# The q projection of the first two token tiles taken from raw x, with LayerNorm applied to its sums

## The chip, the cores and the metric

One core of a Trainium2 chip runs the whole program. Its engines are TensorE (matmul and transpose, "PE"; its weight loads are listed as "PEld"), VectorE ("DVE"), ScalarE ("ACT"), GpSimd ("POOL") and SyncE ("SP", which here issues DMAs). The metric is the device time of one execution in microseconds, from runs on the chip; profiled executions add when each instruction ran.

## The reference

A transformer layer for 2048 tokens of width 1024, in bfloat16: `h = x + attention(LN(x))`, `out = h + gMLP(LN(h))`. What the change touches is the first step:

```python
def _layernorm(x, axis=-1, eps=1e-05):
    m = jnp.mean(x, axis=axis, keepdims=True)
    v = jnp.var(x, axis=axis, keepdims=True)
    return (x - m) / jnp.sqrt(v + eps)

# _A_ref(_layernorm(x), A_wqkv, A_wo): 32 heads of 32, a window of 8 positions in steps of 2
qkv = (x @ wqkv).reshape(B, S, 3, H, Dh)
logits = einsum('bhsd,bhswd->bhsw', q, kg) * Dh ** -0.5
attn = softmax(where(mask, logits, -1e9))
o = einsum('bhsw,bhswd->bhsd', attn, vg)
... o @ wo
```

The LayerNorm has no weights, so for a token with mean m and reciprocal deviation r, q = r * (x @ wq) - (r * m) * (column sums of wq).

## The kernel before

The 2048 tokens are 16 tiles of 128 (`P`), four to a chunk of 512 (`CH`, `TPC` = 4, chunks c = 0 to 3). The inner width 1024 is eight slices kt of 128 (`KT`); the outputs of q, k and v are eight groups dl (`DLO`). TensorE needs x with the width on the partitions, so every normalised tile is transposed: chunk 0 by TensorE (`xpose`, L279), the others by a DMA transpose (L416) from `xns` into `xnT`, of which the pool `xtp` (L191) has two buffers.

At the start (L208 to L238) TensorE runs `NWARM` dummy matmuls on a zeroed tile, while SP's queue loads in this order: half of each of tiles 0 and 1, wq in eight slices of 256 KB with tiles 2 and 3 behind the fifth, two pairs of tiles (2 and 3), wk, pairs 4 and 5, `xl` (the tiles of chunk 3) and wv. ScalarE's queue loads the other halves of tiles 0 and 1 and the constants `csb`: the identity for the transposes, `E32` (used at L527), `B4` (L589) and a mask. Pairs 4 and 5 use the buffers of pairs 0 and 1.

Then comes the first stage, written out in order (L319 to L350). For a tile, VectorE takes the statistics of both halves (`stats`, L241), ScalarE the root (`root`, L264), VectorE the reciprocal (`scale`, L315) and the normalised tile (`norm`, L269). TensorE transposes it, eight blocks of 128 x 128, into PSUM; ScalarE or VectorE copies it to `xnT[0]`. The q of tiles 0 and 1 is summed in two accumulators `qacc` by `q_left(k0, k1, lo, hi)`, for slices k0 to k1 and tiles lo to hi; `ALONE` = 5 slices are done for each tile alone, with 128 columns, while the next tile isn't there yet, and the rest for both, with 256. After L350 the q of tiles 2 and 3 is done with 256 columns (L353 to L358), and ScalarE writes all of it to `att_in[0][0]`, the q of chunk 0.

All that follows is put in order by `Order` (L64): each operation is added with an engine, an estimated duration, what it depends on and a priority, and `run` places them on a clock for each engine; the instructions are emitted in that order, so each engine runs its list in program order whatever the real times are. Its clocks start at the estimated end of the first stage: `{"PE": 22.9, "ACT": 24.1, "DVE": 15.4, "POOL": 12.0}` (L372). `slots` counts the buffers of some tags.

In this list: the LayerNorm of chunks 1 to 3 (`ln1`, L384: statistics on VectorE, a power on GpSimd at L405 for the reciprocal roots, the normalised tiles on VectorE, then the DMA transpose); k and v of chunk 0 and q, k and v of the others (`qkv`, L428, matmuls at L439 in units of four); and `attention` (L461). Attention of chunk 0 starts on VectorE with products of q and k (L497) and three steps of adding (L501, L504, L507). TensorE sums them over the heads' width into the scores with `E32` (L527), and the softmax follows on VectorE and ScalarE. `prod`, `part` and `ssum` are the tags of the tiles used there.

Of the kernel before, what the change touches and what calls it, by code (L numbers as in the profile page):

```python
# [29 lines left out]
EPS = 1e-5  # L30
SCALE = DH ** -0.5
NEG = -1.0e9
NWARM = 11
ALONE = 5
XRB = 3
LMODE = (1, 1, 1, 1)
LSLACK, BSLACK = 2.0, 0.3
# [5 lines left out]


def _consts():
    c = np.zeros((P, 128 + 32 + 128 + 128), np.float32)
    c[:, 0:128] = np.eye(P)
    for p in range(P):
        c[p, 128 + p // 4] = 1.0
    for k in range(P):  # L50
        h = k % 32
        c[k, 160 + 4 * h:160 + 4 * h + 4] = 1.0
    for w in range(W_WIN):
        for s in range(16):
            if s - DIL * w < 0:
                c[0:32, 288 + w * 16 + s] = NEG
    return c.astype(ml_dtypes.bfloat16)


# [68 lines left out]
def kernel(  # L128
# [31 lines left out]
    csb = cpool.tile([P, 416], BF16, name="csb")  # L160
    ident = csb[:, 0:128]
    E32 = csb[:, 128:160]
    B4 = csb[:, 160:288]
    maskb = csb[0:32, 288:416].rearrange("p (w s) -> p w s", w=W_WIN)
# [45 lines left out]
    wps = ps_tp.tile([P, CH], FP32, name="wps", tag="t0")  # L210
    for _ in range(NWARM):
        T.matmul(wps[:], warm[:, 0:P], warm[:], start=True, stop=True)
    V.memset(eps_t[:], EPS)
    V.memset(nhalf[:], -0.5)

    wsb = [wtile([P, KT, D], "wq", "wA"), wtile([P, KT, D], "wk", "wA"), wtile([P, KT, D], "wv", "wB")]
    with tc.manual_schedule(engines={mybir.EngineType.SP}):
        for i in range(TPC):
            x_slot(i)
        for i in range(2):  # L220
            for q_, lo in ((nc.sync, 0), (nc.scalar, CH)):
                q_.dma_start(xts[i][:, lo:lo + CH], x2d[i * P:(i + 1) * P, lo:lo + CH])
        A.dma_start(csb[:], consts_d.ap()[:, :])
        for kt in range(KT):
            dma(wsb[0][:, kt, :], wq_view[:, kt, 0:D])
# [12 lines left out]
        dma(wsb[2][:], wq_view[:, :, 2 * D:3 * D])  # L238
# [33 lines left out]
            V.tensor_scalar(xn[:, lo:hi], xts[i][:, lo:hi], mv1[:, i, 0:1], rstd1[:, i:i + 1], op0=ALU.subtract, op1=ALU.mult)  # L272
# [6 lines left out]
    def xpose(i, lo, hi, tag):  # L279
        ps = (ps_acc.tile([P, 2, 2 * CH], BF16, name="tpa", tag="acc")[:, 0] if tag == "acc" else  # L280
              ps_tp.tile([P, 2 * CH], BF16, name="tp" + tag, tag=tag))
        for a in range(lo, hi):
            T.transpose(ps[:, (a - lo) * P:(a - lo + 1) * P], xn[i][:, a * P:(a + 1) * P], ident)  # L283
        return lambda cp: cp(xnT[0][:, i, lo:hi, :], ps[:, 0:(hi - lo) * P].rearrange("p (a s) -> p a s", s=P))

    def q_mm(dst, dl, kt, lo, hi, start, stop):
        T.matmul(dst.rearrange("p (a b) -> p a b", b=P), wqs[:, kt, dl, :], xnT[0][:, lo:hi, kt, :], start=start, stop=stop)  # L287

    def q_left(k0, k1, lo, hi):
        for kt in range(k0, k1):  # L290
            for dl in range(DLO):
                c0 = (dl % 2) * 2 * P
                q_mm(qacc[dl // 4][:, dl % 4 // 2, c0 + lo * P:c0 + hi * P], dl, kt, lo, hi,
                     kt == 0 and lo == 0 and dl % 2 == 0, kt == KT - 1 and dl % 2 == 1)

    def q_half_out(half, lo, acc):
        A.copy(att_in[0][0][:, 4 * half:4 * half + 4, lo * P:(lo + 2) * P], acc[:].rearrange("p a (d s) -> p (a d) s", d=2))
# [30 lines left out]
    scale(1)
    xn[1] = norm(1, cuts=(0, CH, D))
    q_left(0, ALONE - 1, 0, 1)  # L330
    xpose(1, 0, 4, "t0")(A.copy)
    q_left(ALONE - 1, ALONE, 0, 1)
    xpose(1, 4, 8, "t1")(A.copy)
# [8 lines left out]
    q_left(0, ALONE, 1, 2)
    q_left(ALONE, ALONE + 1, 0, 2)
    xpose(2, 0, 4, "t0")(A.copy)
    xpose(2, 4, 8, "t1")(A.copy)
    q_left(ALONE + 1, KT - 1, 0, 2)
    xpose(3, 0, 4, "t0")(A.copy)
    xpose(3, 4, 8, "t1")(V.tensor_copy)
    q_left(KT - 1, KT, 0, 2)
    sm7 = sums_act(7, 0, junk())  # L350
    for half in range(2):
        q_half_out(half, 0, qacc[half])
    sums_act(7, 1, junk(), sm7)  # L353
    for half in range(2):
# [29 lines left out]
    def ln1(c):  # L384
        sts = []
        for il in range(TPC):
            i = c * TPC + il
            arrive = add("DMA", X_AT[c] + 0.8 * il, lambda: None)
            if il < TPC - 1 or c == 3:
                sts.append(add("DVE", 1.4, lambda i=i: stats(V, i), [arrive], prio=LNPRIO[c]))  # L390
                continue
            if c == 1:
                G["sm", c] = sm7
                sa = add("DMA", 19.0, lambda: None)
            else:
                def sums(i=i):
                    G["sm", c] = sums_act(i, 0, junk())
                    sums_act(i, 1, junk(), G["sm", c])
                sa = add("ACT", 2.4, sums, [arrive], prio=4.0, lat=0.2)
            sts.append(add("DVE", 0.45, lambda i=i: var_act(i, G["sm", c]), [sa], prio=LNPRIO[c]))  # L400
        def ve():
            G["ve", c] = l1.tile([P, TPC], FP32, name="ve1", tag="ve1")
            V.tensor_scalar(G["ve", c][:], mv1[:, c * TPC:(c + 1) * TPC, 1], EPS, None, op0=ALU.add)
        s1 = add("DVE", 0.15, ve, sts, prio=LNPRIO[c] - 0.5)
        r1 = add("POOL", 1.05, lambda: nc.gpsimd.tensor_tensor(rstd1[:, c * TPC:(c + 1) * TPC], G["ve", c][:], nhalf[:], op=ALU.pow),  # L405
                 [s1], lat=0.4)
# [566 lines left out]
```

## Time and profile before

| what | value |
|---|---|
| median of 3 runs | 724.17 us (724.12 to 726.06) |
| the profiled execution | 723.34 us |
| its span, first to last instruction | 721.6 us |
| TensorE's granted clock, mean | 1.000 |
| first real transpose on TensorE | 6.31 us |
| first matmul of k (L439) in the chain | 23.23 us |
| first product of attention 0 on VectorE (L497) | 39.76 us |
| POOL busy in the whole span | 51.2 us |

Times in the timeline are microseconds from the first instruction of the span. A line of it gives the start, the length, the engine, the line of the kernel, the operation and what it writes and reads; a bracket at the end is the idle time of the engine before it and what ended that. Lines of the chain give start, length and what was running. TensorE's matmuls are pipelined, so the length of one is more than the distance to the next; for the rate one divides a run of them by their number.

### The profile page before, as it was taken

What the parts mean: (1) busy time and instruction counts of PE and PEld (TensorE: products, weight loads), DVE (VectorE), ACT (ScalarE), POOL (GpSimd) and SP (SyncE); (2) the same over time, 40 slices, a digit from 0 to 9 for tenths busy, and PEclk for the clock granted to TensorE, in tenths of its full rate; (3) what the DMA queues carried; (4) which work ended last, traced back from release to release, by engine and by line L of the source; (5) the groups of instructions that cost most, each with busy time, mean ns of one, the idle gap of its engine ahead of it and who ended that gap; (6) DMA issues with size and microseconds to landing.
All of it is one profiled execution on the core that took longest, in us unless ns stands there. A gap on an engine that the chain in (4) does not pass through costs nothing.

```text
span 721.6 us, 8559 instructions
## 1 busy us (share of the span) xinstructions
PE 714.1 (99%) x3493; PEld 370.3 (51%) x3537; DVE 420.8 (58%) x470; ACT 217.7 (30%) x280; POOL 51.2 (7%) x61
## 2 busy tenths in 40 slices
PE   8999999999999999999999999999999999999998
PEld 7766665666545444445445444444444444444444
DVE  6899899999999799988951103222222222222222
ACT  4523432533348866738825420000000000000000
POOL 0100010012110111000204100000000000000000
PEclk9999999999999999999999999999999999999999
DMA  9964697389973594642849899163016411120002
GB/s 327 322 185 110 201 215 206 128 233 277 312 301 58 188 238 142 233 117 66 223 129 294 230 299 295 48 148 116 29 45 128 132 33 45 35 86 11 0 17 71
DMA packets 117590, 113.12 MB, mean 157 GB/s; under 512 B 68080, under 2 KB 95120, under 8 KB 117424
## 3 DMA queue, kind: packets, MB, share of 16 engines
q1 hardware_dynamic: 108528, 75.48, 35.7%
q0 software_dynamic: 8448, 36.64, 17.6%
q8 instruction: 27, 0.44, 0.3%
q10 hardware_dynamic: 576, 0.47, 0.2%
q14 instruction: 11, 0.09, 0.0%
HBM read 57.19 MB, written 31.26 MB: 123 GB/s over the span
## 4 chain that ended last, share of the span: by engine, by line
PE 98%; DMA 0%; DVE 0%; issue 0%; ACT 0%
PE acc L912 27%; PE acc L439 21%; PE acc L816 13%; PE acc L761 13%; PE acc L927 13%; PE acc L684 8%; PE acc L287 2%; DMA xp<-in_A_x_dram 0%; PE L L527 0%; PE tpt L283 0%; PE pb L589 0%; DVE bnst L242 0%; DVE xn L272 0%; DVE bnst L243 0%; PE tpa L283 0%
## 5 line engine op out<-in xcount | busy, mean ns | idle before, releaser
L912 PE MATMUL acc<-wspT,z2sb 128*128 128x512 bf16 x878 | 193.1, 379 | 0.9
L912 PEld LDWEIGHTS <-z2sb 128*128 128x128 bf16 x896 | 87.7, 98 | 105.7
L915 DVE TENSOR_TENSOR g<-acc,bB 128x1024 bf16<-128x1024 f32 x28 | 34.3, 1224 | 160.2 <-PE acc L912 127.9
L816 PE MATMUL acc<-hnT,win 128*128 128x512 bf16 x448 | 98.0, 379 | 0.0
L761 PE MATMUL acc<-win,hnT 128*128 128x512 bf16 (+1 forms) x501 | 97.4, 352 | 0.6
L761 PEld LDWEIGHTS <-hnT 128*128 128x128 bf16 x512 | 49.9, 98 | 47.5 <-issue 0.7
L497 DVE TENSOR_TENSOR prod<-qT,kT 128x4096 bf16<-128x4096 bf16 x32 | 72.4, 2283 | 0.0
L927 PEld LDWEIGHTS <-zg 128*128 128x128 bf16 x462 | 44.7, 98 | 52.4
L816 PEld LDWEIGHTS <-win 128*128 128x128 bf16 x448 | 43.7, 98 | 52.6 <-issue 0.7
L450 ACT CAST stg<-acc 128x1024 bf16<-128x1024 f32 x36 | 36.4, 1011 | 77.2 <-PE acc L439 66.4
L934 DVE TENSOR_TENSOR ot<-acc,hr 128x1024 bf16<-128x1024 f32 x15 | 18.4, 1225 | 69.4 <-PE acc L927 60.5
L927 PE MATMUL acc<-wout_a,zg 128*128 128x512 bf16 (+2 forms) x260 | 58.0, 373 | 0.3
L439 PE MATMUL acc<-xnT,wk 128*128 128x512 bf16 x256 | 56.5, 380 | 0.0
L439 PE MATMUL acc<-xnT,wv 128*128 128x512 bf16 x256 | 56.1, 380 | 0.0
L684 PE MATMUL acc<-wo_sb,av_oT 128*128 128x512 bf16 x250 | 55.6, 379 | 0.3
L439 PEld LDWEIGHTS <-wv 128*128 128x128 bf16 x256 | 36.7, 144 | 18.5 <-issue 0.2
L439 PEld LDWEIGHTS <-wk 128*128 128x128 bf16 x256 | 36.6, 144 | 18.7 <-issue 0.7
L927 PE MATMUL acc<-wout_b,zg 128*128 128x512 bf16 (+2 forms) x193 | 43.8, 373 | 0.2
L439 PE MATMUL acc<-xnT,wq 128*128 128x512 bf16 x192 | 42.1, 380 | 0.0
L684 PEld LDWEIGHTS <-av_oT 128*128 128x128 bf16 x256 | 25.0, 98 | 30.1
L822 ACT ACTIVATE z1s<-acc 128x1024 bf16<-128x1024 f32 x28 | 28.6, 1022 | 37.8 <-PE acc L816 33.5
L501 DVE TENSOR_TENSOR prod<-prod 128x2048 bf16<-128x2048 bf16 x32 | 38.4, 1217 | 0.1
(140 smaller groups left out, 562.1 us busy)
## 6 DMA issues: line engine op xcount, KB each, us to landing
qkv_d<-stg SPq DMA_DIRECT2D x36, 256.0 KB, 3.9
z_d<-z1s SPq DMA_DIRECT2D x28, 256.0 KB, 2.6
z1c<-z_d SPq DMA_DIRECT2D x28, 256.0 KB, 2.8
z_d<-u SPq DMA_DIRECT2D x12, 448.0 KB, 2.8
z2sb<-z_d POOLq DMA_DIRECT2D x12, 448.0 KB, 9.7
xr<-in_A_x_dram SPq DMA_DIRECT2D x16, 256.0 KB, 3.1
av_y<-av_z POOLq DMA_DIRECT2D x4, 1024.0 KB, 8.6
av_oT<-av_zz POOLq DMA_DIRECT2D x4, 1024.0 KB, 12.1
```

The source lines that it names most:

```text
L439: T.matmul(G[key][:, j, :].rearrange("p (a b) -> p a b", a=TPC), wv[:, kt, dl, :], xnT[c][:, :, kt, :], start=(kt == 0), stop=(kt == KT - 1))
L450: A.copy(stg[:], G[key][:])
L497: V.tensor_tensor(st["prod"][:], qT[:], kT[:, :, o:o + CH], op=ALU.mult)
L501: V.tensor_tensor(dst, p_[:, 0:4, :], p_[:, 4:8, :], op=ALU.add)
L684: T.matmul(st["acc", il][:, nh, :], oTs[c][:, dl, il * P:(il + 1) * P], wo_sb[:, dl, nh * CH:(nh + 1) * CH], start=(dl == 0), stop=(dl == ...
L761: T.matmul(accf[:, n0:n1], hnTs[c][:, il, kt, :], wins[hf][:, kt, n0:n1], start=(kt == 0), stop=(kt == KT - 1))
L816: T.matmul(G["accy", c, fp][:, j, :].rearrange("p (a b) -> p a b", a=TPC), wt[:, kt, f0 * P:(f0 + 1) * P], hnTs[c][:, :, kt, :], start=(kt ...
L822: A.activation(z1s[:], G["accy", c, fp][:], ACTF.Gelu_apprx_tanh)
L912: T.matmul(acc[:, j, :], z2sb[a][:, f * P:(f + 1) * P], wspT[:, a, :], start=(a == 0), stop=(a == NT - 1))
L915: V.tensor_tensor(g1[:], acc[:], bB[:, c * CH:(c + 1) * CH].unsqueeze(1).to_broadcast([P, 2, CH]), op=ALU.add)
L927: T.matmul(outs, zg[:, f, il * P:(il + 1) * P], wt[:, f0, lo:hi], start=(f == 0), stop=(f == NF - 1))
L934: V.tensor_tensor(ot[:], acc[:].rearrange("p a b -> p (a b)"), hr[:], op=ALU.add)
```

## The change

The constants lose the identity, which GpSimd now makes in place (a memset and an affine_select). `NWARM` goes from 11 to 6, `ALONE` from 5 to 2. The first tile comes in two halves on two queues as before; the second in one piece on SP's queue, behind the first slice of wq; the constants behind all of wq.

Tiles 0 and 1 are transposed as they come, into a tile `raw`, and the q of both is summed from it. They are normalised later and transposed again into `xT0`, which serves k and v. Their means and reciprocal deviations are written to DRAM and read back as rows, repeated on all partitions, in `mr`; all of these DMAs are on GpSimd's queue. ScalarE copies the sums to `qraw`. GpSimd multiplies mean by deviation, and `qraw` by the deviation. `xT0` has a column of ones behind the last token, so the q matmuls of tiles 2 and 3, 257 columns wide, also give wq's column sums (`csum`). Two operations in the ordered list, one for each half, multiply these with `mr[:, 0]` and subtract that from `qraw`, both on GpSimd, into `att_in[0][0]`.

`raw` and `xT0` are two tiles of the tag `xnT`, and `qraw` and `qcor` two of the tag `part`.

```diff
-NWARM = 11
-ALONE = 5
+NWARM = 6
+ALONE = 2
+XC = TPC * P + 4
...
+    nc.gpsimd.memset(ident[:], 0.0)
+    nc.gpsimd.affine_select(out=ident[:], in_=ident[:], compare_op=ALU.not_equal, fill=1.0, base=0, pattern=[[-1, P]], channel_multiplier=1)
...
-        for i in range(2):
-            for q_, lo in ((nc.sync, 0), (nc.scalar, CH)):
-                q_.dma_start(xts[i][:, lo:lo + CH], x2d[i * P:(i + 1) * P, lo:lo + CH])
-        A.dma_start(csb[:], consts_d.ap()[:, :])
+        for q_, lo in ((nc.sync, 0), (nc.scalar, CH)):
+            q_.dma_start(xts[0][:, lo:lo + CH], x2d[0:P, lo:lo + CH])
         for kt in range(KT):
             dma(wsb[0][:, kt, :], wq_view[:, kt, 0:D])
+            if kt == 0:
+                dma(xts[1], x2d[P:2 * P, :])
...
+        dma(csb[:], consts_d.ap()[:, :])
...
-    xnT[0] = xtp.tile([P, TPC, KT, P], BF16, name="xnT", tag="xnT")
+    xT0 = xtp.tile([P, KT, XC], BF16, name="xT0", tag="xnT")
+    V.memset(xT0[:, :, TPC * P:TPC * P + 1], 1.0)
+    xnT[0] = xT0[:, :, 0:TPC * P].rearrange("p a (t s) -> p t a s", s=P)
+    raw = xtp.tile([P, KT, XC], BF16, name="raw", tag="xnT")
...
+    def q_left(kt, lo, hi):
+        for dl in range(DLO):
+            c0 = (dl % 2) * 2 * P
+            T.matmul(qacc[dl // 4][:, dl % 4 // 2, c0 + lo * P:c0 + hi * P], wqs[:, kt, dl, :], raw[:, kt, lo * P:hi * P],
+                     start=(kt == 0 and lo == 0 and dl % 2 == 0), stop=(kt == KT - 1 and dl % 2 == 1))
...
-    stats(V, 0)
-    scale(0)
-    xn[0] = norm(0, cuts=(0, 2 * P, CH, D))
...
+    qacc.extend((new_acc(), new_acc()))
+    put = [xpose(xts[0], raw, 0, lo, lo + 4, tag) for lo, tag in ((0, "t0"), (4, "t1"))]
+    put[0](V.tensor_copy)
+    put[1](A.copy)
+    stats(V, 0)
+    q_left(0, 0, 1)
+    xpose(xts[1], raw, 1, 0, 4, "t0")(A.copy)
+    q_left(1, 0, 1)
+    xpose(xts[1], raw, 1, 4, 8, "t1")(A.copy)
     stats(V, 1)
...
+    sd0 = root(0, 2)
+    V.reciprocal(rstd1[:, 0:2], sd0[:, 0:2])
+    st_d = dpool.tile([2, 2 * P], FP32, name="st_d")
+    dma_w(st_d[0].rearrange("(t p) -> p t", p=P), mv1[:, 0:2, 0])
+    dma_w(st_d[1].rearrange("(t p) -> p t", p=P), rstd1[:, 0:2])
+    mr = att.tile([P, 2, 2 * P], FP32, name="mr", tag="ssum")
+    for k in range(2):
+        dma_w(mr[:, k, :], st_d[k].unsqueeze(0).to_broadcast([P, 2 * P]))
+    xn[0], xn[1] = norm(0), norm(1)
+    q_left(0, 1, 2)
+    q_left(1, 1, 2)
+    q_left(2, 0, 2)
+    q_left(3, 0, 2)
+    for i, tag in ((0, "t0"), (1, "t1")):
+        xpose(xn[i], xT0, i, 0, 8, tag)(A.copy)
+        q_left(4 + i, 0, 2)
     stats(V, 2)
     sd2 = root(2, 3)
...
+    q_left(6, 0, 2)
+    xpose(xn[2], xT0, 2, 0, 8, "t0")(A.copy)
+    q_left(7, 0, 2)
+    xpose(xn[3], xT0, 3, 0, 4, "t1")(V.tensor_copy)
+    xpose(xn[3], xT0, 3, 4, 8, "t0")(V.tensor_copy)
+    qraw = att.tile([P, DLO, 2 * P], FP32, name="qraw", tag="part", bufs=2)
+    qcor = att.tile([P, DLO, 2 * P], FP32, name="qcor", tag="part", bufs=2)
+    csum = l1.tile([P, DLO], FP32, name="csum", tag="csum")
+    for half in range(2):
+        A.copy(qraw[:, 4 * half:4 * half + 4, :], qacc[half][:].rearrange("p a (d s) -> p (a d) s", d=2))
+    nc.gpsimd.tensor_tensor(mr[:, 0, :], mr[:, 0, :], mr[:, 1, :], op=ALU.mult)
+    nc.gpsimd.tensor_tensor(qraw[:], qraw[:], mr[:, 1, :].unsqueeze(1).to_broadcast([P, DLO, 2 * P]), op=ALU.mult)
     sm7 = sums_act(7, 0, junk())
...
+    for dp in range(DLO // 2):
         acc = new_acc()
+        for j in range(2):
             for kt in range(KT):
+                T.matmul(acc[:, j, 0:2 * P + 1], wqs[:, kt, 2 * dp + j, :], xT0[:, kt, 2 * P:4 * P + 1], start=(kt == 0), stop=(kt == KT - 1))
+        A.copy(att_in[0][0][:, 2 * dp:2 * dp + 2, 2 * P:4 * P], acc[:, :, 0:2 * P])
+        A.copy(csum[:, 2 * dp:2 * dp + 2], acc[:, :, 2 * P])
+        if dp == 0:
+            sums_act(7, 1, junk(), sm7)
...
-    o_ = Order({"PE": 22.9, "ACT": 24.1, "DVE": 15.4, "POOL": 12.0}, {"acc": 3, "L": 1, "prod": 1, "part": 2, "xn": 4})
+    o_ = Order({"PE": 21.4, "ACT": 22.6, "DVE": 15.4, "POOL": 18.5}, {"acc": 3, "L": 1, "prod": 1, "part": 0, "xn": 4})
...
     def attention(c):
         if c == 0:
-            d_q = add("DMA", 24.2, lambda: None)
+            mean_ = mr[:, 0, :].unsqueeze(1).to_broadcast([P, 4, 2 * P])
+            for half, at_ in ((0, 21.6), (1, 24.0)):
+                d4 = slice(4 * half, 4 * half + 4)
+                def cor(d4=d4):
+                    nc.gpsimd.tensor_tensor(qcor[:, d4], csum[:, d4].unsqueeze(2).to_broadcast([P, 4, 2 * P]), mean_, op=ALU.mult)
+                    nc.gpsimd.tensor_tensor(att_in[0][0][:, d4, 0:2 * P], qraw[:, d4], qcor[:, d4], op=ALU.subtract)
+                d_q = add("POOL", 3.0, cor, [add("DMA", at_, lambda: None)], free="part", lat=0.3)
```

More of the change, by code (lines that the diff above doesn't have):

```diff
@@ L45, in _consts @@
 def _consts():
-    c = np.zeros((P, 128 + 32 + 128 + 128), np.float32)
-    c[:, 0:128] = np.eye(P)
+    c = np.zeros((P, 32 + 128 + 128), np.float32)
     for p in range(P):
-        c[p, 128 + p // 4] = 1.0
+        c[p, p // 4] = 1.0
     for k in range(P):
         h = k % 32
-        c[k, 160 + 4 * h:160 + 4 * h + 4] = 1.0
+        c[k, 32 + 4 * h:32 + 4 * h + 4] = 1.0
     for w in range(W_WIN):
@@ L55, in _consts @@
             if s - DIL * w < 0:
-                c[0:32, 288 + w * 16 + s] = NEG
+                c[0:32, 160 + w * 16 + s] = NEG
     return c.astype(ml_dtypes.bfloat16)
@@ L159 @@
     cpool = ctx.enter_context(tc.tile_pool(name="consts", bufs=1))
[L160 to L164, printed above, removed]
+    csb = cpool.tile([P, 288], BF16, name="csb")
+    ident = cpool.tile([P, P], BF16, name="ident")
+    E32 = csb[:, 0:32]
+    B4 = csb[:, 32:160]
+    maskb = csb[0:32, 160:288].rearrange("p (w s) -> p w s", w=W_WIN)
     eps_t = cpool.tile([P, 1], FP32, name="eps_t")
@@ L273, in norm, with xpose @@
         return xn
-    xnT[0] = xtp.tile([P, TPC, KT, P], BF16, name="xnT", tag="xnT")
+    xT0 = xtp.tile([P, KT, XC], BF16, name="xT0", tag="xnT")
+    V.memset(xT0[:, :, TPC * P:TPC * P + 1], 1.0)
+    xnT[0] = xT0[:, :, 0:TPC * P].rearrange("p a (t s) -> p t a s", s=P)
+    raw = xtp.tile([P, KT, XC], BF16, name="raw", tag="xnT")
     xns = {c: bp.tile([P, TPC, D], BF16, name=f"xns{c}", tag=f"hn{c - 1}", bufs=1) for c in (1, 2)}
-    def xpose(i, lo, hi, tag):
-        ps = (ps_acc.tile([P, 2, 2 * CH], BF16, name="tpa", tag="acc")[:, 0] if tag == "acc" else
-              ps_tp.tile([P, 2 * CH], BF16, name="tp" + tag, tag=tag))
+    def xpose(src, dst, i, lo, hi, tag):
+        ps = ps_tp.tile([P, 2 * CH], BF16, name="tp" + tag, tag=tag)
         for a in range(lo, hi):
[L283 to L297, printed above, removed]
+            T.transpose(ps[:, (a - lo) * P:(a - lo + 1) * P], src[:, a * P:(a + 1) * P], ident[:])
+        return lambda cp: cp(dst[:, lo:hi, i * P:(i + 1) * P], ps[:, 0:(hi - lo) * P].rearrange("p (a s) -> p a s", s=P))
+    def q_left(kt, lo, hi):
[3 more added lines that the diff above has]
+                     start=(kt == 0 and lo == 0 and dl % 2 == 0), stop=(kt == KT - 1 and dl % 2 == 1))
     att_in = {}
@@ L320 @@
     A.activation(wsq[:], eps_t[:], ACTF.Sqrt)
+    qacc.extend((new_acc(), new_acc()))
+    put = [xpose(xts[0], raw, 0, lo, lo + 4, tag) for lo, tag in ((0, "t0"), (4, "t1"))]
+    put[0](V.tensor_copy)
+    put[1](A.copy)
     stats(V, 0)
-    scale(0)
-    xn[0] = norm(0, cuts=(0, 2 * P, CH, D))
-    for put in [xpose(0, lo, hi, tag) for lo, hi, tag in ((0, 2, "t0"), (2, 4, "t1"), (4, 8, "acc"))]:
-        put(A.copy)
-    qacc.extend((new_acc(), new_acc()))
-    stats(V, 1)
[L328 to L333, printed above, removed]
+    q_left(0, 0, 1)
+    xpose(xts[1], raw, 1, 0, 4, "t0")(A.copy)
+    q_left(1, 0, 1)
+    xpose(xts[1], raw, 1, 4, 8, "t1")(A.copy)
+    stats(V, 1)
+    sd0 = root(0, 2)
[14 more added lines that the diff above has]
+        q_left(4 + i, 0, 2)
     stats(V, 2)
@@ L341 @@
     xn[3] = norm(3, cuts=(0, CH, D))
[L342 to L349, printed above, removed]
+    q_left(6, 0, 2)
[10 more added lines that the diff above has]
+    nc.gpsimd.tensor_tensor(qraw[:], qraw[:], mr[:, 1, :].unsqueeze(1).to_broadcast([P, DLO, 2 * P]), op=ALU.mult)
     sm7 = sums_act(7, 0, junk())
[L351 to L354, printed above, removed]
+    for dp in range(DLO // 2):
         acc = new_acc()
-        for j in range(4):
+        for j in range(2):
             for kt in range(KT):
-                q_mm(acc[:, j // 2, (j % 2) * 2 * P:(j % 2 + 1) * 2 * P], 4 * half + j, kt, 2, TPC, kt == 0, kt == KT - 1)
-        q_half_out(half, 2, acc)
+                T.matmul(acc[:, j, 0:2 * P + 1], wqs[:, kt, 2 * dp + j, :], xT0[:, kt, 2 * P:4 * P + 1], start=(kt == 0), stop=(kt == KT - 1))
[3 more added lines that the diff above has]
+            sums_act(7, 1, junk(), sm7)
     ps_tp_stack.close()
@@ L414, in tr @@
         def tr():
-            xnT[c] = xtp.tile([P, TPC, KT, P], BF16, name="xnT", tag="xnT")
-            i_ = nc.sync.dma_start_transpose(xnT[c][:].rearrange("p il a s -> p (il a) s"), xns[c][:].rearrange("s il (a p) -> s (il a) p", p=P))
+            xb = xtp.tile([P, KT, XC], BF16, name="xnT", tag="xnT")
+            xnT[c] = xb[:].rearrange("p a s -> p (a s)")[:, 0:TPC * D].rearrange("p (t a s) -> p t a s", t=TPC, a=KT)
+            i_ = nc.sync.dma_start_transpose(xb[:].rearrange("p a s -> p (a s)")[:, 0:TPC * D].rearrange("p (k s) -> p k s", s=P), xns[c][:].rearrange("s il (a p) -> s (il a) p", p=P))
             if c == 3:
```

## The prediction

> **What bounds the kernel now.** I read the page's engine totals and chain first, then the waits of TensorE, then the chain and the timeline of the first 24 us, then the places where TensorE meets VectorE and GpSimd again. Page, engine totals and chain:
>
> ```profile
> PE 714.1 (99%) x3493; PEld 370.3 (51%) x3537; DVE 420.8 (58%) x470; ACT 217.7 (30%) x280; POOL 51.2 (7%) x61
> PE 98%; DMA 0%; DVE 0%; issue 0%; ACT 0%
> ```
>
> TensorE's waits over the whole span, longest in all:
>
> ```profile
> PE wps L212 <- DVE eps_t L213: 1.2, 1, 1.2
> PE tpt L283 <- DVE xn L272: 1.0, 1, 1.0
> ```
>
> So nothing can be won but TensorE work or these two waits, and any new wait of TensorE is paid in full. The chain of the first stage (start, length):
>
> ```profile
> 0.74 2.80 DMA xp<-in_A_x_dram
> ...
> 3.57 0.69 DVE bnst L242
> ...
> 6.31 0.38 PE tpt L283 x4
> ...
> 13.58 0.45 PE tpt L283 x8
> ...
> 15.36 7.87 PE acc L287 x72
> 23.23 36.91 PE acc L439 x171
> ```
>
> Tile 0 lands at 3.55, its LayerNorm takes until 6.28, TensorE works from 6.31 without a gap. The change attacks the 2.7 us between. Where the score sums (L527) stand, timeline (start, length):
>
> ```profile
> 73.28 0.75 DVE L507 TENSOR_TENSOR part<-prod 128x512 bf16<-128x512 bf16 x2
> 74.96 0.61 PE L527 MATMUL L<-part,csb 128*32 128x512 bf16 x8
> ```
>
> Their input is ready at 74.03, so TensorE gets there 0.93 late: VectorE's spare time against a hand-written order.
>
> **TensorE work.** Removed: five dummy matmuls (hidden behind the load of x, 0.43 each while the clock is at half speed). Added: tiles 0 and 1 are transposed twice, 16 more transposes at 0.45 per 8 = +0.9. Moved: 48 matmuls of 128 columns (kt 2, 3, 4) become 24 of 256: 32 narrow ones took 2.09, 0.065 each; 72 wide ones 7.87, 0.109 each; 48 x 0.065 - 24 x 0.109 = -0.5. The column of ones makes 64 matmuls 257 wide instead of 256: under 0.03 in all. Net +0.4, against up to 2.7 of earlier start.
>
> **The early start, walked through.** The six dummies end at 1.19 + 6 x 0.43 = 3.77. Tile 0 is there at 3.55. The identity now comes from GpSimd: a memset (rows of 0.10 to 0.12) and an affine_select, which no row shows; between 0.1 (a memset) and 1.04 (GpSimd's power of 4 columns) I take 1, ready by 2 and hidden; it shows only beyond 2.5. The eight transposes run at half clock, 0.9, as the dummies kept 0.43 apart until 4.5. VectorE copies the first half (0.42, its PSUM copy row of 128x512) to 4.9. wq's first piece: before, 872 KB (tiles 0 and 1, constants, wq 0) had landed at 1.67 + 4.2 = 5.87. Now 512 KB stand up to it, 360 KB less at 390 GB/s: 4.95. In the same way tile 1 lands at 5.6, wq 1 at 6.3, wq 2 at 6.9, always 0.66 apart; flow in the trace would allow 0.45 less. So: kt 0 of tile 0 to 5.5, four transposes of tile 1 to 5.9, wait for wq 1, kt 1 to 6.8, four transposes to 7.05, kt 0 and 1 of tile 1 (16 x 0.065) to 8.1, kt 2 and 3 (16 x 0.109) to 9.85. VectorE meanwhile: two statistics from 4.9 (1.53 each) to 8.0, root 0.29, reciprocal 0.17, normalised tiles 0 and 1 (0.55 each) by 9.7. They are just in time: transposes to 10.3, kt 4 to 11.15, transposes of tile 1 to 11.6, kt 5 and 6 to 13.35. At 9.85 TensorE stands about 1.5 ahead of the old kernel.
>
> **Where it goes.** ScalarE works in program order, and the root of tile 2 now stands behind its copy of normalised tile 1 (1024 wide; 0.59 for 512 and 1.01 for 1024 from the rows, I take 1.0): 11.8 to 12.8. Root 13.15, reciprocal 13.35, normalise 13.9 (old: 12.05). TensorE waits 0.55. Transposes to 14.4, kt 7 to 15.3. VectorE: second half of tile 3's statistics and aggregate to 14.75, root, reciprocal, normalise in two cuts of 0.37 to 15.7 and 16.05 (old: 14.33). TensorE waits 0.4, transposes four, and now has no matmuls left to cover VectorE's copies (the old kernel had kt 7, 0.87): copies to 16.5 and 16.95. The 64 matmuls of tiles 2 and 3 start at 16.55 (old: 16.23) and end 7.0 later, 23.55, against 23.23: **+0.3**. With the earlier landings it is 22.9, -0.35. I take +0.2. The lead of 1.5 is spent on +0.9 of transposes and on four waits (wq 1, tile 2, tile 3, its copy).
>
> **Other parts that cost nothing, and their cover.** The constants (72 KB) go behind wq on SP; first use is L527 at 75. On SP, the load of pair 5 waits for the readers of tile 3 (14.33, now 16.0), xl and wv behind it: wv landed at 15.5 + 16.8 = 32.3 and is used at 36.9, so 1.7 leaves 2.9. ScalarE gets four narrow copies of sums and four evictions of 512 columns instead of two of 1024; it has 0.3 to 2.4 of idle time at each accumulator; three accumulators are enough, since each is freed at least one group (1.75) before it is needed.
>
> **GpSimd's part.** Four DMAs issued at its queue after rstd (8.5): two writes, then two broadcasts that wait for the writes. Issue 0.75 to 1.26 (rows), landing 2.5 to 8.6 (the 32 KB stores): complete between 15 and 29; queued behind are both products and the power of chunk 1 (L405). I take 16, before the sums are ready: ScalarE's two copies of them (1.0 each, after tile 2's copy) end at 18.3. Then the product of 2048 fp32 columns, price p. No row has it. Below: VectorE does 512 fp32 columns in 0.65 (L546), 2.5 for 2048. Above: 2.5 stretched as GpSimd's power was, 1.04 to 2.93 when it ran beside VectorE's two-input products (timeline):
>
> ```profile
> 20.83 1.04 POOL L405 TENSOR_TENSOR rstd<-ve,nhalf 128x4 f32<-128x4 f32 x1 [20.38 <-DVE ve L403]
> 345.45 2.93 POOL L657 TENSOR_TENSOR l3rstd<-l3var,nhalf 128x4 f32<-128x4 f32 x1 [1.90 <-DVE l3var L653]
> ```
>
> That is 7.0. On 4 columns GpSimd multiplies in 0.20 to 0.25 (L659), VectorE in 0.16 (L651), up to 1.55 as long: I take p = 3.9, near the lower row. Then the corrections cost 2p in four products. The power of chunk 1 (20.83 before; its input now 1.1 later, 21.9, because VectorE's copies end later) runs at max(21.9, 18.3 + p) = 22.2; the power of chunk 2 (29.24 before) stands behind the corrections, in time 18.3 + p + 1.05 + 2p = 31.05. VectorE has only one statistic of 1.4 to fill with, the rest of LayerNorm and attention 0 queue behind it, so attention 0 starts D = 3p - 9.9 = 1.8 late (39.76 before). Its spare time at L527: 0.93, + 0.2 from TensorE, + what the new order gives. That order was computed with TensorE at 21.4 instead of 22.9, but I have it at 23.4: in units of four matmuls, L527 moves back by one or two, 0.86 to 1.73. Threshold 2.0 to 2.9: **0** to pay.
>
> The Trainium skill (GPSIMD Engine Reference, Performance versus the Vector engine) gives 4497 ns for a two-input fp32 product of 2048 columns on GpSimd, and 2293 on VectorE, which agrees with 4 x 0.65 here; by it p = 4.5, D = 3.6 and the sum would be 0.7 to 1.6 more.
>
> **Sum.** 723.34 (the profiled execution; span 721.6 and 1.7 around it) + 0.2 = 723.5; the median of the runs is 0.83 above that execution, so **724.4** beside 724.17.
>
> **Rivals.**
> GpSimd becomes the bound (slower). Place: TensorE at L527, waiting for VectorE, which waited at the chunk 2 power behind the corrections. Price 3p - 9.9 less 2.0 to 2.9, from p = 4.0 to 4.3 on; p = 4.5 gives 725.6, p = 7.0 (8.2 to 9.1 paid) 733. Broadcasts landing after 18.3 add to it one for one. For: three large products stand in front of a power that VectorE waits for, and the 2.93 row. Against: statistics are what VectorE mostly runs there, and the stretched rows stood beside two-input products. The skill (SBUF — State Buffer, SBUF: two separate sides) calls the port pair an exclusive lock held for the whole instruction, and the 2.93 agrees that GpSimd waits; whether a long GpSimd product holds VectorE up no row here shows.
>
> The lead survives: tile 2's root isn't held, VectorE's tail ends as it did (15.8), the 64 matmuls start at 15.1 to 15.6, after TensorE's own work. 0.7 to 1.1 is gained: 723.3. For: 1.5 of lead at 9.85. Against: ScalarE's order.
>
> Buffer of xnT: two buffers, now taken by the normalised and the raw tile. If chunk 1's transpose gets the normalised one, it waits for the last v matmul (50.5) instead of starting at 23.84, and TensorE waits for it, 4.9 (second transpose) to 10.7 (first): 731. Against: the raw one is free by 15.3.
>
> The change doesn't do what it says: the identity comes late, each us after 3.8 shifts the start; 2 us gives 726.
>
> **Chances.** Forecast 0.48, GpSimd 0.30, lead 0.10, buffer 0.07, identity 0.05. Forecast's own range 723.6 to 725.2. The range of 8 in 10 is 722.8 to 728.5: out fall half of the lead (0.05), the buffer, and GpSimd beyond 4 (0.08). About 0.3% (2.2 us) is what a measurement tells from no change: slower by more takes half of GpSimd, the buffer and part of the identity, 0.25; faster would need TensorE without any new wait, 0.03; the rest, 0.72, is within.
>
> **What would show it.** Right: first real transpose at 3.8; TensorE waiting about 0.5 on tiles 2 and 3 with tile 2's root behind ScalarE's copy; first L439 matmul at 23.0 to 23.6; no TensorE wait at L527. Wrong: L439 starting by 22; GpSimd products over 4.3 and a TensorE wait on VectorE near 76; a transpose of chunk 1 at 50; a first transpose after 5.

## The result, and the profile after

| | median, us | lowest to highest | runs |
|---|---|---|---|
| before | 723.88 | 723.27 to 726.06 | 6 |
| after | 743.36 | 742.67 to 744.55 | 6 |
| ratio | 1.0267 | 95% interval 1.0251 to 1.0283 | |

The change costs 19.5 us, where 0.2 was forecast. The span of the profiled execution grows from 721.6 to 741.1, again by 19.5, so the trace can be asked where all of it went. After, page: engine totals and the shares of the chain that ended last.

```profile
PE 718.1 (97%) x3477; PEld 371.5 (50%) x3524; DVE 428.5 (58%) x469; ACT 218.3 (29%) x283; POOL 70.3 (9%) x73
...
PE 87%; DVE 8%; DMA 2%; POOL 1%; issue 1%; DVEq 0%; POOLq 0%
```

Before, TensorE was 98% of that chain. Now 13% of it stands with others. TensorE's waits after (us in all, times, longest):

```profile
PE L L549 <- DVE part L529: 10.2, 1, 10.2
PE acc L455 <- DMA wk<-in_A_wqkv_dram: 3.6, 1, 3.6
PE wps L212 <- DVE eps_t L215: 1.2, 1, 1.2
PE tpt L288 <- DVE xn L275: 0.7, 2, 0.4
PE acc L294 <- DMA wq<-in_A_wqkv_dram: 0.7, 1, 0.7
PE acc L370 <- ACT csum L372: 0.4, 1, 0.4
```

Two waits are new and large: 10.2 at the score sums (L549, L527 before) and 3.6 for wk. The small ones are the first stage's. The places in TensorE's timeline after (start, length; the bracket is the wait), and the granted clock behind the two long waits (from a view by windows: window, its length, then each engine's busy time, then TensorE's granted clock, DMA share and GB/s):

```profile
4.08 0.83 PE L288 MATMUL tpt<-ident,xp 128*128 128x128 bf16 x8
...
17.23 5.47 PE L370 MATMUL acc<-xT,wq 128*128 128x257 bf16 x48 [0.20 <-DVE xT L289]
...
28.61 0.65 PE L455 MATMUL acc<-xT,wk 128*128 128x512 bf16 x1 [3.62 <-DMA wk<-in_A_wqkv_dram]
...
92.74 0.62 PE L549 MATMUL L<-part,csb 128*32 128x512 bf16 x4 [10.20 <-DVE part L529]
```

```profile
28.60:32.00 3.40, 3.17 (x8) 1.39 (x10) 0.00 (x0) 0.00 (x0) 3.40 (x1) 0.51 1.05 388
...
92.70:97.00 4.30, 4.26 (x14) 1.68 (x14) 3.25 (x6) 1.23 (x2) 0.00 (x0) 0.53 0.56 197
```

The start of k in the same view of before:

```profile
23.07 2.10 PE L439 MATMUL acc<-xnT,wk 128*128 128x512 bf16 x9
```

The account: k starts at 28.61 instead of 23.07, +5.5 (1.9 from a later q stage, 3.6 for wk). Then 3.4 us at a clock of 0.51, 3.4 x 0.49 = 1.7 lost. Then 10.2 at L549. Then 4.3 us at 0.53, 2.0 lost. Together 19.4 of 19.5. Both long waits are paid twice: once as idle time, once as half speed behind it.

What was late for L549 is read from the chain of waits after, from the first statistics on (start, length):

```profile
7.75 0.22 DVE mv L247
7.97 0.30 issue
8.27 0.86 POOL st_d L332
9.13 0.04 issue
9.17 11.76 DMA st_d<-rstd
20.93 0.28 issue
21.22 6.20 DMA mr<-st_d
...
28.25 4.53 POOL qraw L364
32.78 1.02 POOL rstd L420
33.79 0.03 issue
33.82 9.18 DVE xns L275 x4
```

The write of 1 KB takes 11.76, the broadcast 6.20, the product of 2048 columns 4.53; only then comes the power of chunk 1 (L420), at 32.73 in GpSimd's timeline instead of 20.83. And four normalised tiles of chunk 1 take 9.18, for which before needed 1.92 (timeline of before):

```profile
21.90 1.92 DVE L272 TENSOR_SCALAR xns<-xp,mv,rstd 128x1024 bf16<-128x1024 bf16 x4 [1.16 <-POOL rstd L405]
```

The first product of attention 0 starts at 55.47 instead of 39.76, and VectorE's last part is ready at 92.68 instead of 74.03.

Two readings stand side by side for the rest: how much of the 19.5 comes from the **transfers** of the mean and deviation rows, how much from GpSimd's **products**, and for each by which mechanism.

### The profile page after: what moved, and what is told of

The parts are those of the page before. It is cut to its first block, busy times and chain, and to the rows that moved or that the text cites. A ratio compares the mean times of both kernels' runs of the same rounds, so it can differ in the third digit from the quotient of the medians.

```text
span 741.1 us, 8548 instructions
## 1 busy us (share of the span) xinstructions
PE 718.1 (97%) x3477; PEld 371.5 (50%) x3524; DVE 428.5 (58%) x469; ACT 218.3 (29%) x283; POOL 70.3 (9%) x73
## 4 chain that ended last, share of the span: by engine, by line
PE 87%; DVE 8%; DMA 2%; POOL 1%; issue 1%; DVEq 0%; POOLq 0%
PE acc L934 26%; PE acc L455 14%; PE acc L838 13%; PE acc L783 13%; PE acc L949 13%; PE acc L706 7%; DVE prod L519 2%; DVE xns L275 2%; DMA st_d<-rstd 2%; DVE prod L523 1%; DMA mr<-st_d 1%; DVE bnst L246 1%; DVE bnst L245 1%; DVE prod L526 1%; POOL qraw L364 1%
## 5 line engine op out<-in xcount | busy, mean ns | idle before, releaser
L455 PE MATMUL acc<-xnT,wk 128*128 128x512 bf16 x192 | 44.2, 390 | 0.0
L455 PE MATMUL acc<-xnT,wv 128*128 128x512 bf16 x192 | 42.2, 379 | 0.0
## 6 DMA issues: line engine op xcount, KB each, us to landing
av_oT<-av_zz POOLq DMA_DIRECT2D x4, 1024.0 KB, 11.8
```

The costliest lines, as they stand in the source:

```text
L455: T.matmul(G[key][:, j, :].rearrange("p (a b) -> p a b", a=TPC), wv[:, kt, dl, :], xnT[c][:, :, kt, :], start=(kt == 0), stop=(kt == KT - 1))
```

## The experiments

Times of each group are compared with runs of the kernel before on the same chip (medians 723.37 to 723.53). Line numbers of the experiments differ by a few from those of after; the names are the same.

| experiment | median, us | ratio to before, 95% interval |
|---|---|---|
| rows set, no transfers | 733.60 | 1.0144 (1.0128 to 1.0159) |
| transfers, no products | 732.26 | 1.0120 (1.0102 to 1.0138) |
| neither | 724.41 | 1.0012 (1.0003 to 1.0021) |
| rows written in one piece | 738.15 | 1.0201 (1.0186 to 1.0216) |
| rows set, products in pieces | 728.54 | 1.0065 (1.0052 to 1.0078) |
| rows set, products moved in the list | 733.74 | 1.0137 (1.0121 to 1.0154) |
| rows set, products made to wait | 728.09 | 1.0055 (1.0033 to 1.0077) |
| neither, tile 2's root first | 723.39 | 0.9995 (0.9987 to 1.0004) |
| whole, rows by TensorE, pieces | 731.73 | 1.0131 (1.0098 to 1.0164) |
| whole, rows by TensorE, waits | 743.88 | 1.0283 (1.0261 to 1.0305) |
| the same, kt 7 split | 749.22 | 1.0334 (1.0306 to 1.0362) |

### Transfers or products

**Rows set, no transfers.** The five statements that write the rows to DRAM and read them back go; `mr` is set once at the start.

```diff
-    st_d = dpool.tile([2, 2 * P], FP32, name="st_d")
...
-        dma_w(mr[:, k, :], st_d[k].unsqueeze(0).to_broadcast([P, 2 * P]))
+    V.memset(mr[:], 1.0)     # beside the other memsets at the start
```

> The rows of mean and deviation (mr) are set to ones by VectorE at the start; their two writes to DRAM and two broadcasts are left out, so q of tiles 0 and 1 isn't normalised. Theory A (the 4-byte pieces of the two writes slow all other loads and make mr late): wk lands at 21 to 23 instead of 28.6, no TensorE wait for it (3.6) and no half clock after it (1.7); the product of qraw starts at 18.4 instead of 28.25, VectorE's part is 9.8 earlier (82.9), TensorE would be at the score sums at 76.8 and wait 6; total 743.4 - 9.8 = 733.5. Theory B (the loads are late through the order on SP's queue, whose pair loads wait for VectorE): wk still lands after 27 and the waits of 3.6 and 1.7 stay; the total is 733 to 734 as well, so the trace decides.

**Transfers, no products.** The DMAs stay; `qraw`, `qcor` and all GpSimd products go, ScalarE writes the sums straight to `att_in[0][0]`.

```diff
-        A.copy(qraw[:, 4 * half:4 * half + 4, :], qacc[half]...)
-    nc.gpsimd.tensor_tensor(qraw[:], qraw[:], mr[:, 1, :]..., op=ALU.mult)
+        A.copy(att_in[0][0][:, 4 * half:4 * half + 4, 0:2 * P], qacc[half]...)
...
-                    nc.gpsimd.tensor_tensor(qcor[:, d4], csum[:, d4]..., mean_, op=ALU.mult)
-                    nc.gpsimd.tensor_tensor(att_in[0][0][:, d4, 0:2 * P], qraw[:, d4], qcor[:, d4], op=ALU.subtract)
+                    pass
```

> GpSimd's products and corrections are left out: ScalarE copies the raw sums of tiles 0 and 1 straight to q; the four DMAs stay. Theory A and B: wk lands at 28.6 and is waited for as in the changed kernel (3.6 and 1.7 of half clock). The power of chunk 1 runs at about 24.4 when its input is there but still behind the four DMAs on the queue (mr issued by 21.8), the score sums' wait of 10.2 and 1.9 of half clock behind it go: 743.4 - 12.1 = 731.3. If the loads, not the products, make VectorE late, the wait at the score sums stays above 3.

**Neither.** Both edits at once: what is left is the early start.

> Both are left out: no rows of mean and deviation, no products. What is left is the early start on raw x with its second set of transposes. If A and the products are all there is: k starts at 24.9 against 23.1, no wait at the score sums, 723.9 + 1.8 = 725.7. If B: k starts at 28.6 and about 731.

Measured: 733.60, 732.26 and 724.41, for an expected 733.5, 731.3 and 725.7. TensorE's long waits with the rows set, and with the transfers alone:

```profile
PE L L545 <- DVE part L525: 7.0, 1, 7.0
```

```profile
PE acc L451 <- DMA wk<-in_A_wqkv_dram: 3.4, 1, 3.4
```

So transfers alone cost 7.85 over the early start, products alone 9.2, both 19.0, 2 more than their sum. With the transfers alone, TensorE waits 3.4 for wk and not at the score sums; k starts at 28.34 in the chain instead of 24.39, +4.0, and the first 240 matmuls from there take 54.80 instead of 51.80, +3.0: all of the 7.0 between the two spans (729.8 and 722.8). With the products alone there is no wait for wk and one of 7.0 at the score sums, with half clock behind it (0.50 from 83 to 88). Each wait belongs to one cause. The 2 more come where the two meet: with late rows the power of chunk 1 runs at 32.73, without them at 23.25. The early start itself costs 1.0; that is taken up below.

In the kernel without transfers, GpSimd's and VectorE's timelines at chunk 1's normalised tiles:

```profile
24.28 1.89 POOL L479 TENSOR_TENSOR qcor<-csum,mr 128x1024 f32<-128x1024 f32 x1
26.25 2.44 POOL L480 TENSOR_TENSOR qT<-qraw,qcor 128x1024 bf16<-128x1024 f32 x1
28.64 2.08 POOL L479 TENSOR_TENSOR qcor<-csum,mr 128x1024 f32<-128x1024 f32 x1
30.80 2.43 POOL L480 TENSOR_TENSOR qT<-qraw,qcor 128x1024 bf16<-128x1024 f32 x1
```

```profile
24.33 9.18 DVE L275 TENSOR_SCALAR xns<-xp,mv,rstd 128x1024 bf16<-128x1024 bf16 x4 [1.16 <-POOL rstd L416]
```

Four products and four tiles begin together and end together (33.23 and 33.51). The tiles are cheap, 0.5 each, but each one waits for a product to end: in narrower windows of the same view the tiles end at 26.45, 28.96, 31.00 and 33.51, each 0.27 or 0.28 behind the end of a product (26.17, 28.69, 30.72 and 33.23). The 9.18 is thus the length of GpSimd's work, not of VectorE's.

### How the transfers hurt: the pieces

The write takes one value from each partition: 256 pieces of 4 bytes. This kernel writes the same 1 KB from one partition's row; `rows` is set, so q is corrected with ones; the first write is issued at 9.22 instead of 8.27.

```diff
-    dma_w(st_d[0].rearrange("(t p) -> p t", p=P), mv1[:, 0:2, 0])
-    dma_w(st_d[1].rearrange("(t p) -> p t", p=P), rstd1[:, 0:2])
+    rows = att.tile([P, 2, 2 * P], FP32, name="rows", tag="attn")
+    V.memset(rows[0:1], 1.0)
+    for k in range(2):
+        dma_w(st_d[k:k + 1, :], rows[0:1, k, :])
```

> The two writes to DRAM carry as many bytes, 1 KB each, but from one partition in a row (set to ones) instead of 4 bytes from each of 256 places; all else stays, q of tiles 0 and 1 isn't normalised. If the small pieces are what is slow: the writes land in 2 to 4 us instead of 11 to 12, DMA keeps 380 GB/s from 14 to 20 us, and the times are those of the run with the rows set, 733 to 735. If any write to DRAM by GpSimd's queue does it: landing 11 to 12 and 743.

The view of transfers for the first 40 us (GB/s in slices of 1 us, then issues: KB each, median us to landing), after:

```profile
GB/s 0 23 245 317 270 305 334 356 381 404 390 391 378 312 109 47 29 55 98 195 152 319 379 352 340 299 389 401 389 395 387 387 389 371 387 385 360 111 35 0
...
wk<-in_A_wqkv_dram SPq DMA_DIRECT2D x1, 2048.0 KB, 18.8
...
mr<-st_d POOLq DMA_DIRECT2D x2, 128.0 KB, 6.3
...
st_d<-mv POOLq DMA_DIRECT2D x1, 1.0 KB, 11.1
st_d<-rstd POOLq DMA_DIRECT2D x1, 1.0 KB, 11.8
```

Before, and then the rows in one piece:

```profile
GB/s 0 12 244 352 268 346 391 367 391 395 404 393 389 401 365 383 389 387 383 389 389 387 385 383 389 389 375 389 385 380 215 44 277 177 188 295 221 402 150 262
...
wk<-in_A_wqkv_dram SPq DMA_DIRECT2D x1, 2048.0 KB, 12.7
```

```profile
GB/s 0 5 248 390 301 393 389 348 326 393 376 372 410 405 373 389 387 385 408 354 385 379 381 385 393 385 387 381 379 387 287 63 20 0 0 0 0 0 45 214
...
wk<-in_A_wqkv_dram SPq DMA_DIRECT2D x1, 2048.0 KB, 13.2
...
st_d<-rows POOLq DMA_DIRECT2D x2, 1.0 KB, 5.8
```

With 4-byte pieces all loads fall from near 390 to between 29 and 195 GB/s from 14 to 21 us; with one piece of the same bytes they don't, and wk lands as it did before (12.7 from its issue before, 13.2 here, 18.8 after). The wait for wk is gone. That the writes in small pieces starve the loads is shown; the number of pieces, their size and the partitions that they come from change together here, so which of these counts, and how, inside the DMA engines, no run here shows. The time of 738.15 is 3 to 5 above what was expected, since I had the rows ready at 18: writes 5.8 and broadcasts 5.3 bring them at 21.84, the product starts at 22.55, and the wait at the score sums is 11.3. Beside the run with the rows set, the product starts 4.5 later (18.06 there), and the wait is 4.3 longer. The rows' lateness thus decides too, not only the loads.

### How the products hurt: held tiles, and place in the queue

All three have the rows set, without transfers, and are compared with 733.60.

**Products in pieces** of 256 columns.

```diff
-    nc.gpsimd.tensor_tensor(qraw[:], qraw[:], mr[:, 1, :].unsqueeze(1).to_broadcast([P, DLO, 2 * P]), op=ALU.mult)
+    for d in range(DLO):
+        nc.gpsimd.tensor_tensor(qraw[:, d], qraw[:, d], mr[:, 1, :], op=ALU.mult)
...     # the corrections likewise, for each d of a half
```

> As the run with the rows set (no DMAs for them), and GpSimd's products cut into 8 and 16 pieces of 256 columns, the same arithmetic. Theory A (a GpSimd product holds VectorE's normalise up for the whole instruction): each of chunk 1's four normalised tiles waits for one piece of about 0.6 instead of one of 1.9 to 2.4, 9.18 becomes 3 to 5, the wait at the score sums falls from 7.0 to 1 to 3, 733.6 becomes 727 to 729. Theory B (the four are slow because all of GpSimd's work has to be done first, or because of something else that runs then, loads or ScalarE): 9.2 stays or grows by the pieces' overhead, 733 to 735.

728.54: the four tiles take 3.33 instead of 9.18, although the scaling as such got longer (5.59 instead of 4.61).

```profile
24.45 3.33 DVE L275 TENSOR_SCALAR xns<-xp,mv,rstd 128x1024 bf16<-128x1024 bf16 x4 [1.16 <-POOL rstd L417]
```

The wait at the score sums falls from 7.0 to 2.5.

**Products moved in the list** only: an entry for the last normalised tile of chunk 1 added to what the corrections depend on, which the planner uses for its order.

```diff
-                d_q = add("POOL", 3.0, cor, [add("DMA", at_, lambda: None)], free="part", lat=0.3)
+                d_q = add("POOL", 4.4, cor, [add("DMA", at_, lambda: None), G["normed", 1]], free="part", lat=0.3)
```

> As the run with the rows set, and the corrections put behind chunk 1's normalised tiles in the ordered list. Theory A: the four take 1.92 again, the corrections run from 26 to 35 beside statistics, which don't wait; the power of chunk 2, ready near 31, waits for them until 35; VectorE is 5 to 6 late instead of 9.2, the wait at the score sums 3 to 4: 729.5 to 731. Theory B: the four still take over 5, and 733.

733.74, a miss: on the chip the products ran from 24.31 on as before and the tiles took 9.17. GpSimd's own order was the same already, and a place in a list makes no engine wait for another. It says nothing on the theories.

**Products made to wait** on the chip, by a dependence of the first product of each half on the last normalised tile of chunk 1.

```diff
+                    i_ = nc.gpsimd.tensor_tensor(qcor[:, d4], ...)
+                    tc.add_manual_dep(i_.ins, norm_ins[4 * after + 3].ins.name, wait_for, ...)
```

> As the run with the rows set, with a semaphore wait of the corrections for chunk 1's last normalised tile, which the run that only moved them in the list did not have. Theory A (a product holds a normalised tile up, and a power waits in the queue behind the products): chunk 1's four take 1.92 from 24.3, the corrections 26.3 to 35.2, chunk 2's power runs at 35.2, VectorE is 3.4 earlier than in the run with the rows set, the wait at the score sums 3 to 4: 729.5 to 730.5. Theory B (not the products hold the four up): they take over 5 again, 733.

```profile
26.31 1.91 DVE L277 TENSOR_SCALAR xns<-xp,mv,rstd 128x1024 bf16<-128x1024 bf16 x4 [1.16 <-POOL rstd L418]
```

```profile
28.40 1.89 POOL L481 TENSOR_TENSOR qcor<-csum,mr 128x1024 f32<-128x1024 f32 x1 [2.12 <-DVE xns L277]
```

The same products, whole and as long, but behind the tiles instead of beside them: the tiles are back at 1.91 and the time at 728.09, 5.5 below 733.60 and 1.4 below what was expected. That settles the holding: it is the overlap that costs, not the products' length. A wait of 2.3 is left at the score sums; the power of chunk 2 stands behind the corrections, at 37.35 in GpSimd's timeline (29.24 before), the place in the queue that the prediction had named. In this profile some 2.0 of that lateness is the first stage's: k started at 25.95, with the rows only set at 23.94, since TensorE ran slow for longer behind the six dummies (32 narrow matmuls in 3.69 instead of 2.91). The other three runs, 727.14 to 729.07, lie about it, so it doesn't carry the verdict.

### The early start alone

The kernel with neither starts k at 24.23 (23.07 before) and takes 1.0 longer. Its suspected cost is tile 2's root behind ScalarE's copy. Here tile 2's statistics and root are written ahead of the copy of normalised tile 1; the rest as in the kernel with neither.

```diff
-    for i, tag in ((0, "t0"), (1, "t1")):
-        xpose(xn[i], xT0, i, 0, 8, tag)(A.copy)
-        q_left(4 + i, 0, 2)
-    stats(V, 2)
-    sd2 = root(2, 3)
+    xpose(xn[0], xT0, 0, 0, 8, "t0")(A.copy)
+    stats(V, 2)
+    sd2 = root(2, 3)
+    q_left(4, 0, 2)
+    xpose(xn[1], xT0, 1, 0, 8, "t1")(A.copy)
+    q_left(5, 0, 2)
```

> As the run with neither rows nor products (the early start alone, q of tiles 0 and 1 not normalised), and tile 2's statistics and root put ahead of ScalarE's copy of normalised tile 1. Theory A (the early start's lead is spent on ScalarE's order): tile 2's root runs at 12.1 instead of 13.24, the 64 matmuls of tiles 2 and 3 start at 16.1 instead of 17.17, k at 23.2 to 23.4 instead of 24.4: 1.0 to 1.2 less, 723.3. Theory B (VectorE's chain through tile 3 sets it anyway): under 0.4 less, 724 to 724.4.

ScalarE and the 64 matmuls of tiles 2 and 3, without and with the edit:

```profile
12.33 1.01 ACT L289 COPY xT<-tpt 128x1024 bf16<-128x1024 bf16 x1 [0.32 <-PE tpt L288]
13.24 0.30 ACT L269 ACTIVATE sd<-mv,eps_t 128x1 f32<-128x1 f32 x1
...
17.17 7.22 PE L360 MATMUL acc<-xT,wq 128*128 128x257 bf16 x64 [0.20 <-DVE xT L289]
```

```profile
11.77 0.30 ACT L269 ACTIVATE sd<-mv,eps_t 128x1 f32<-128x1 f32 x1
12.19 1.01 ACT L289 COPY xT<-tpt 128x1024 bf16<-128x1024 bf16 x1
...
15.99 7.23 PE L361 MATMUL acc<-xT,wq 128*128 128x257 bf16 x64
```

The 64 start at 15.99 instead of 17.17, k at 23.06, and the time is 723.39 beside 723.53, ratio 0.9995 (0.9987 to 1.0004). The order of two ScalarE instructions was the whole loss of the early start; and without it the early start is level with before. Nothing is won to pay for rows and products.

### Mending the whole

Three kernels compute all of it again. The rows come without DRAM: a column of `stb` (mean times deviation, and deviation, in bfloat16), repeated 128 times with a stride of zero as one operand, times the identity, gives a row on all partitions; four matmuls and one ScalarE copy.

```diff
+    for k in range(4):
+        T.matmul(rp[:, k * P:(k + 1) * P], stb[:, k:k + 1].to_broadcast([P, P]), ident[:], start=True, stop=True)
+    A.copy(mr[:].rearrange("p a b -> p (a b)"), rp[:])
```

Tile 2's root is first. The first version adds the products in pieces and new starting clocks for the planner:

> The whole computation, mended: the rows of mean times deviation and deviation made by four TensorE matmuls of a column repeated 128 times with the identity, and one ScalarE copy; tile 2's root ahead as in the run before; GpSimd's products in pieces of 256 columns; the first half of the corrections behind chunk 1's normalised tiles, the second behind chunk 2's; the planner's clocks at 23.0, 24.0, 16.4 and 21.9. If A holds: rows by 11, scaling done by 22, powers and normalised tiles within 1 us of the old times, no wait at the score sums, k at 23.4: 723 to 724.5, level with the kernel before. If the products still hold VectorE up: 726 or more.

The second has whole products that wait for the last normalised tile of chunks 1 and 2, and the clocks of after:

> The whole computation: rows of mean times deviation and deviation by TensorE and ScalarE as in the first mended version, tile 2's root ahead, the planner's clocks of the changed kernel, whole products, and a semaphore wait of the first half of the corrections for chunk 1's last normalised tile and of the second for chunk 2's. Theory A (GpSimd's products cost only where they meet VectorE's normalised tiles and powers): chunk 1's and 2's normalised tiles take 1.9 each, VectorE is at most 1.3 late at the score sums, TensorE waits under 0.7 there, k at 23.3: 723.5 to 724.5. If the products slow VectorE's statistics too: over 726.

The third is the second with kt 7 split around tile 3's transposes:

> As the mended version with the waits, and the last slice of the first two tiles (kt 7) split: half of its matmuls before the transposes of tile 3's first half, half between that and the second. If VectorE's copies are what the 64 matmuls wait for: they start at 15.6 instead of 16.0, k 0.4 earlier, 723.1 to 724.1. If TensorE's own order already covers it: no change.

All three miss: 731.73 (731.39 to 740.17), 743.88 and 749.22 (744.29 to 750.33; its profile is of the fastest run). Their first stages are as wished. In the first, the rows cost TensorE 0.22 (8.59 to 8.81), but the four tiles of chunks 1 and 2 take 3.04 and 3.09 beside the pieces, VectorE waits 1.40 for a load of x, and TensorE waits 1.9 at the score sums and another 4.9 later. In the second k starts at 23.30, the tiles take 1.92 and 1.86, and TensorE doesn't wait at the score sums; all its new waits stand later:

```profile
PE acc L711 <- DVE av_oT L648: 7.8, 3, 4.0
PE acc L459 <- ACT stg L470: 7.2, 1, 7.2
```

That is 15.0. Behind two of these waits the granted clock is 0.50: 16 matmuls take 6.41 instead of 3.67 and 64 take 15.66 instead of 13.98, another 4.4. With k 0.2 later it makes 19.6 of the 20.6 between the spans (742.2 and 721.6). VectorE is 2.6 late at the end of attention 0's products (76.99, and 74.35 in the kernel with neither and the root first): a tiny operation still takes 1.36 beside the scaling product and the power of chunk 3 3.08. The only large difference I found between there and the waits: a 128 KB store of the attention weights is issued at 85.16, behind a 1 MB load issued at 84.13, and lands after 6.3; before, the store went at 82.75, ahead of the load at 82.99, and landed after 2.4. That this order is the cause of the later waits is argued from the timeline; no run tried it. In the third, the split moves the start of the 64 matmuls only from 16.21 to 15.99, k starts at 23.31 as in the second, and the waits are 8.7 and 6.0.

No version beat the kernel before.

## Why the prediction was wrong

Three steps of the sum failed: the rows were taken as ready at 16 and came at 27.42, the transfers had no price for the loads in flight, and a VectorE held by GpSimd's products was left at nothing. By the runs, the transfers alone cost 7.85 and the products alone 9.2 over the early start's 1.0.

**What held.** The first real transpose was forecast at 3.8 and came at 4.08; the identity was to be ready by 2 and was at 1.31 (0.20 and 0.29 for its two instructions). Tile 2's root behind ScalarE's copy: forecast to end at 13.15, ended at 13.60, with waits of 0.32 and 0.38 on tiles 2 and 3 for 0.55 and 0.4. The constants behind wq and the load of wv show no wait; the smaller evictions, costed at nothing, held TensorE once for 0.4, but only with the transfers: ScalarE had waited 2.96 for a late load of x ahead of them. Chunk 1's transpose did not wait for the last v matmul, so the rival of the buffers fell.

**The rows: "I take 16".** The bounds for the four DMAs were 15 to 29; 27.42 was measured. The step that failed is choosing the near end. The price was taken from 32 KB stores, and the shape of the write, 256 pieces of 4 bytes, was left out of account: the two writes landed after 11.1 and 11.8, beyond the 8.6 that was the far end for one. Even in one piece the rows came at 21.84, behind the 18.3 at which the sums were to be ready. It cost twice. The scaling product started at 28.25 instead of 18.3, and the wait of the rival then grew, as the prediction had said, with late broadcasts.

**wk: no term at all.** The sum priced the four DMAs by when their own data comes, and never asked what they do to the loads in flight. wk had come 12.7 after its issue in before, and k waited for nothing. After, it came 18.8 after its issue: 3.6 of waiting and 1.7 of half clock. With the transfers alone the kernel is 7.85 slower than with neither.

**The held tiles: left at nothing.** The prediction said that no row shows whether a long GpSimd product holds VectorE up, bounded nothing by it, and let VectorE run its tiles beside the corrections in 1.92. They took 9.18. The Trainium skill (SBUF — State Buffer, SBUF: two separate sides) says that a GpSimd instruction and a VectorE instruction that needs the shared ports too (one in a 2-port mode, or with two inputs in SBUF) exclude each other: whichever starts first has these ports for its whole instruction, and the other stands still. It was cited in the prediction for GpSimd's side alone. The traces agree for VectorE's side too, 9.18 beside the products and 1.91 when they wait; in which mode the tiles run, no view shows. So the unknown had a bound: four tiles, one held for each product, 2p = 7.8 by the prediction's own p.

**The products' price p.** Taken as 3.9, measured 4.53; the corrections 8.84 (1.89 + 2.44 + 2.08 + 2.43) for 2p. The Trainium skill (GPSIMD Engine Reference, Performance versus the Vector engine) has 4497 ns for a two-input fp32 `tensor_tensor` of 2048 columns (an add), which this agrees with; VectorE's row of 512 columns was a poor guide. Its 2293 for VectorE, which the prediction called in agreement, is 12% under the 2.6 of 4 x 0.65. The error is 0.6 on p and 1.0 on the corrections, small beside the others.

**"L527 moves back by one or two units": it didn't.** It stands behind the same 48 matmuls of k in both kernels, so the threshold was too generous by 0.86 to 1.73.

**The early start: +0.2, measured +1.0.** The working itself gave +0.3, with wq 1 at 6.3 (TensorE got it at 6.91 after, 6.84 in the kernel with neither) and the 64 matmuls from 16.55 (17.17 with neither). "With the earlier landings it is 22.9" pulled the choice the wrong way. The mechanism, the root behind the copy, was right: without it the 64 start at 15.99. The rival "the lead survives" had its condition met there, but not its price: it put the 64 at 15.1 to 15.6 and the gain at 0.7 to 1.1, and k at 23.06 is level with before.

**The rival.** "GpSimd becomes the bound" had the place, TensorE at the score sums, and the queue, but 0.7 to 9 us for a chance of 0.30. It had only the queue. With rows at 27.42, the held tiles, and the half clock behind each wait, the same mechanism comes to 10.2 + 2.0, and wk to another 5.3. Late rows and a held VectorE were mentioned there as something that might be added; each had a bound in the rows shown (29 for the transfers, 2p for the tiles) and belonged into the sum.

## What to carry to other kernels

Price a small DMA by its pieces and by what else is in flight, and ask of every added transfer what it does to loads that the bounding engine is about to need. When work goes to GpSimd, list the VectorE instructions that will run beside it: each may stand for the length of a whole GpSimd instruction (the normalised tiles did, the statistics didn't), so short pieces or a real wait, not a place in a list, decide what it costs. And a long stall of TensorE can cost more than its own length: behind every one of 6 us and more here, and behind most of 2.5 to 4, it ran at half clock for a time, so add that to the price.

## What the runs showed of the hardware

- Two writes of 256 pieces of 4 bytes, 1 KB each, landed after 11.1 and 11.8 us and held all loads to 29 to 195 GB/s for some 7 us; as one row each they landed after 5.8, with no dip.
- Not only normalised tiles are held. A VectorE product of one element per partition (`sm<-mv`, 0.16 before) took 1.24 to 1.36 beside the scaling product; statistics (0.68) took as long as ever.
- Behind waits of 3.6 and 10.2 (after), 3.4 (transfers alone), 7.0 (rows set) and 11.3 (one piece), TensorE ran at a granted clock of 0.50 to 0.53 for 3.4 to 6 us. Behind 2.5 (products in pieces) it did so too, for some 3.4, but not behind 2.3 (products made to wait), nor behind one of 4.0 in the whole kernel with waits. The Trainium skill (TensorE: Matmul & The Clock Gate, What's actually happening) describes half rate after a window of about 3.4 us of idleness. The long waits agree with it; the 2.5 and the 4.0 show that the length of a wait alone doesn't tell.
- Four matmuls with a repeated column as one operand turned per-partition values into rows on all partitions in 0.22 us of TensorE's time and one ScalarE copy of 0.59, in bfloat16, against 18.3 from the second write's issue to the broadcast's landing.
